# A fused attention and mixer kernel: the table of positions that sets its order, with other numbers

## The chip, the cores and the metric

The kernel runs on 1 core of one Trainium2 chip. The metric is the device time in microseconds (us) of one execution. The kernel before was timed three times: 1544.9, 1541.44 and 1538.11 us, a median of 1541.44 us. The profiled execution is a separate one, and its own time stands in the table below.

## The reference

What must be computed, for 8 batches of 448 positions, 12 heads of 64 and a model width of 768:

```python
scores = matmul(q, k.T) / sqrt(64) - log(448)
attn   = sigmoid(scores)
x      = concat_heads(matmul(attn, v))          # 448 x 768 per batch
h      = x.T @ U @ V                            # rank 32, mixes the positions
u      = x + h.T
out    = u + relu(u @ w_ch1) @ w_ch2            # 768 -> 3072 -> 768
```

There is no softmax, so scores, sigmoid and values of a pair of heads follow each other without a reduction over the row.

## The kernel before, in words

**Attention** of a batch is done in six pairs of heads (`pair`). Scores are matmuls at L578 and, for the last 64 rows of two pairs together, at L582. ScalarE (ACT) takes the sigmoid from PSUM at L706. The values are matmuls at L597 and L607, and VectorE (DVE) copies them out at L752. Batches 0 to 3 and 7 take the scores in float32, the others as pairs of float16 numbers; for those a scale is found by sending two columns to memory and back (`far`, `row`).

**Mixing** (`mix`, `mix_half`): the largest value of three columns of tiles is reduced on DVE (`mm_x`), spread over the partitions by a TensorE transposition (L451), made into a scale by short DVE instructions, and the columns are split into two float16 parts on ACT, GpSimd (POOL) and DVE (`xst`). One DMA transposes them (L893, `xst<-xst`), seven matmuls multiply by U (L901), ACT and DVE take the result (`xnt`), and three matmuls multiply by V (L911).

**The feed-forward part** of batches 0 and 1 (`ffn_in`, `ffn_out`) runs over six groups of hidden columns. A chain of 18 matmuls at L990 makes one tile of hidden values, ACT reads it twice (L997 and L998, relu), DVE takes the difference (L999), and chains of 12 matmuls at L1010 multiply by the second matrix. The weights come as 64-bit numbers. `decode` turns each of the 12 weight blocks into two float16 parts: four DMAs, several DVE and ACT instructions for each of four pieces (L432, L435, L484, L495), a largest value (`mm_w`, L919) that TensorE spreads (L451), and conversions by ACT or POOL (L959) and DVE (L435). The 12 `mm_w` transpositions on TensorE are called **marks** 1 to 12 below. Here mark 3 is the first with the name `mm_w__173`, and a later one has that name again, since three buffers are used in turn.

**Batches 2 to 7** are multiplied in pairs by a scheme of seven products instead of eight, all at L1198.

**The order** is made by a planner when the program is built. Every operation is put down with an engine, a cost, the operations that it needs, and a position `pos`. `Plan.order` then goes forward in planned time: at each step the engine that can begin first takes, of the operations that are ready, the one with the smallest position. Each engine executes its instructions in that order and waits in place where one isn't ready. Positions are sums of the constants at L66 to L74: where a batch's attention starts against the feed-forward groups (`BEFORE`, `AHEAD`, `LATER_AT`), how far values trail scores (`VALUES`, `SECOND`), where the mixing stands (`MIXED`, `MIX_2`), and how far decoding runs ahead (`DECODE`). Buffers are handed out in the planned order too. Two constants are not positions: `BOND` is an advantage in position for a TensorE operation that goes on in the array tiling in use (full, 64 rows, 64 columns, or 64 by 64), and `LATE` is added to the time at which the operations of attention and mixing count as ready on TensorE (for the feed-forward chains it is 0.3).

The line that makes an operation ready, `x[5]` being that slack:

```python
at = told + x[5] if x[0] != e or e == "SP" else end[i] + (0.0 if e == "PE" else 0.14)
```

Of the kernel before, what the change touches and what calls it, by code (L numbers as in the profile page):

```python
# [58 lines left out]
LATER = [2, 3, 4, 5, 6, 7]  # L59
FORMS = {1: (0, 1, 2)}  # L60
MM = 0.1893
SWITCH, BOND = 0.11, 41.647
T32_N = 3
PIPE, LANDS, LATE = 0.32e6, 3.237, -3.383

ROOM0, ROOM, AHEAD, BEFORE, PACE = 181.648, 286.578, -68.264, 91.805, 0.05  # L66
LATER_AT = 266.225
PREP, BOUNDS, VALUES, SECOND, MIXED = 137.851, 20.1, -1.552, 1.83, -5.728
MIXED1, MIX_1 = 4.915, 99.976
MIX_2, EV_IN, EV_OUT, A_OFF = 111.691, 64.755, 39.267, -86.102  # L70
START, DECODE = 280.941, 151.107
U_AT, U_STEP = 14.793, 3.625
LEAD, SUMS, STEP_K, STEP_I, FFN_LEAD = 17.258, 175.507, 40.462, 27.17, -42.823
W_AT, W_STEP, PAIR0, MIX0A, MIX0B, W2_LAG, G0_LEAD = -164.381, 28.657, 21.251, 146.75, -434.739, 1.269, 6.128  # L74
LOW_G = 1
FB = 8
SHIFT = dict()
# [165 lines left out]
def fused_kernel(ctx: ExitStack, tc: tile.TileContext, q, k, v, wu, wv, w1, w2, out):  # L243
# [1079 lines left out]
    def units(n):  # L1323

        b = min(n // NG, PLAIN - 1)
        step = (BEGIN[b + 1] - BEGIN[b]) / NG
        at = BEGIN[b] + (n - b * NG) * step
        nf = ne = 0
        for x in PATTERN:
            if x == "i":  # L1330
                if n < len(slots):
                    ffn_in(*slots[n], nf, at)
                nf += 1
                at += step * 18 / 144
            else:
                if n:
                    ffn_out(*slots[n - 1], ne, at)
                ne += 1
                at += step * 12 / 144

    def attention(b, start, d):
        new_u(b)
        for p in range(NP):
            pair(b, p, start + d * p, d)
            if b >= WHOLE and p in (3, 5):
                mix_half(b, p // 5, start + (MIXED - 5 + p) * d)
        if b < WHOLE:
            mix(b, 0.0, start + MIXED1 * d)

    for n, (b, g) in enumerate(slots):  # L1350
# [15 lines left out]
        if n == NG - 1:  # L1366
            d = PACE * (BEGIN[1] - BEGIN[0]) / 7.6
            attention(1, BEGIN[0] - BEFORE, d)
            d = (BEGIN[PLAIN] - AHEAD - BEGIN[0] - LATER_AT) / (NP * len(LATER) + 0.5)
            for j, x in enumerate(LATER):  # L1370
                attention(x, BEGIN[0] + LATER_AT + NP * d * j, d)
            attended = [len(plan.ops) - 1]
            FORMS_AT, FORMS_STEP = BEGIN[0] + LATER_AT + NP * d * U_AT, U_STEP
    units(len(slots))
# [88 lines left out]
```

## Time and profile before

| what | before |
|---|---|
| median of three runs | 1541.44 us |
| the profiled execution's own time | 1536.72 us |
| its span, first to last instruction | 1534.9 us |
| mean granted TensorE clock | 0.998 |
| DVE, ACT, POOL busy, share of the span | 67%, 43%, 19% |
| mean busy share of the DMA engines' time, queue 1 | 62.6% |

The profiled execution takes 1.8 us more than its span. Matmuls are pipelined, and their ends are modelled, so busy time of TensorE (PE) says when it has something in the array, not that it is at its peak. One matmul with 448 columns of float16 starts 189 ns after the one before it where nothing interferes; a float32 matmul stands as two records in the trace and as one row in the order. "Idle before" in a row is time in which the engine stood still just before it, with what ended that.

### The profile page before, as it was taken

The numbers are of one execution on the slowest core, as the hardware profiler recorded it, in microseconds if no ns is written. First come the engines' busy times: TensorE is split into PE (matmuls) and PEld (weight loads), VectorE is DVE, ScalarE is ACT, GpSimd is POOL, SyncE is SP. The second block draws the span as 40 slices with busy tenths as digits, with TensorE's granted clock in tenths as the row PEclk, the third lists the DMA queues.
The fourth block names the chain that finished last, engine by engine and source line by source line (L and its number), as shares of the span: only waits on it lengthen the run. The fifth ranks groups of instructions, "written<-read, shape, count | busy, mean of one in ns | idle before, by whom it ended". The sixth has DMA issues, their size and how long they took to land.

```text
span 1534.9 us, 22014 instructions
## 1 busy us (share of the span) xinstructions
PE 1512.8 (99%) x8194; PEld 731.6 (48%) x8194; DVE 1030.8 (67%) x1788; ACT 662.9 (43%) x1060; POOL 287.6 (19%) x352
## 2 busy tenths in 40 slices
PE   8999999999999999999999999999999999999999
PEld 3344544434444444445555555555555555555554
DVE  3789887755577756468776768665656757565656
ACT  5677787454465656434242352421223413121310
POOL 0100000444565220002546452000000400000000
PEclk9999999999999999999999999999999999999999
DMA  8788778985877997686766576533335373433331
GB/s 226 244 253 261 281 241 312 296 267 165 198 219 195 236 215 200 215 242 231 249 226 226 191 244 207 181 120 103 119 116 187 117 256 119 123 119 109 108 108 73
DMA packets 202188, 299.18 MB, mean 195 GB/s; under 512 B 52832, under 2 KB 158944, under 8 KB 199008
## 3 DMA queue, kind: packets, MB, share of 16 engines
q1 hardware_dynamic: 202080, 297.77, 62.6%
q8 instruction: 64, 1.05, 0.3%
q14 instruction: 44, 0.36, 0.1%
HBM read 226.20 MB, written 63.23 MB: 189 GB/s over the span
## 4 chain that ended last, share of the span: by engine, by line
PE 90%; DMA 5%; DVE 2%; ACT 2%; issue 1%; SPq 0%; ACTq 0%
PE banks L1198 56%; PE banks L1010 9%; PE banks L990 9%; PE banks L597 6%; PE banks L578 5%; PE banks L607 1%; PE banks L582 1%; DMA xst<-xst 1%; PE banks L901 1%; DMA far<-ss__203 1%; ACT a L706 1%; DMA row__110<-far 1%; DMA qk__99<-k_in 1%; DMA w<-w_in 1%; DMA forms<-xnt 1%
## 5 line engine op out<-in xcount | busy, mean ns | idle before, releaser
L1198 PEld LDWEIGHTS <-w__89 128*128 128x128 f16 x1197 | 117.1, 98 | 109.1
L1198 PEld LDWEIGHTS <-w__91 128*128 128x128 f16 x1134 | 111.0, 98 | 104.1 <-issue 0.8
L1198 PEld LDWEIGHTS <-w__90 128*128 128x128 f16 x1134 | 111.0, 98 | 103.5
L1198 PEld LDWEIGHTS <-w__92 128*128 128x128 f16 x1071 | 104.8, 98 | 97.8
L706 ACT ACTIVATE a<-banks,bias_s 128x896 f32<-128x896 f32 x105 | 99.1, 1007 | 58.9 <-PE banks L578 58.9
L1054 POOL TENSOR_TENSOR w<-w 128x384 f32<-128x384 f32 x96 | 102.0, 1063 | 5.2
L1010 PE MATMUL banks<-h__94,w__92 128*128 128x448 f16 x432 | 86.2, 353 | 0.0
L1010 PE MATMUL banks<-h__93,w__91 128*128 128x448 f16 x432 | 85.9, 353 | 0.0
L990 PE MATMUL banks<-us__87,w__90 128*128 128x448 f16 x432 | 85.0, 353 | 0.5 <-DVE ub__82 L435 0.5
L990 PE MATMUL banks<-us__87,w__89 128*128 128x448 f16 x432 | 84.9, 353 | 0.0
L1050 POOL TENSOR_TENSOR w<-w 128x384 f32<-128x384 f16 x48 | 45.2, 971 | 120.2 <-DVE xnt L1062 88.2
L1010 PEld LDWEIGHTS <-w__91 128*128 128x128 f16 x432 | 41.1, 98 | 45.2 <-issue 8.1
L1010 PEld LDWEIGHTS <-w__92 128*128 128x128 f16 x432 | 41.3, 98 | 44.0 <-issue 7.4
L990 PEld LDWEIGHTS <-w__90 128*128 128x128 f16 x432 | 41.6, 98 | 42.6 <-issue 5.7
L990 PEld LDWEIGHTS <-w__89 128*128 128x128 f16 x432 | 41.6, 98 | 40.7 <-issue 3.6
L1198 PE MATMUL banks<-a,w__89 128*128 128x448 f16 x267 | 60.2, 352 | 0.0
L1198 PE MATMUL banks<-a,w__91 128*128 128x448 f16 x255 | 56.7, 352 | 0.0
L1198 PE MATMUL banks<-a,w__90 128*128 128x448 f16 x249 | 56.2, 352 | 0.0
L1198 PE MATMUL banks<-a,w__92 128*128 128x448 f16 x237 | 53.5, 352 | 0.0
L1155 POOL TENSOR_TENSOR h__94<-w 128x448 f32<-128x448 f32 x2 | 2.3, 1138 | 256.6 <-ACT xst L1158 256.1
L435 DVE SCALAR_TENSOR_TENSOR stg<-w,stg 128x768 int32<-128x768 int32 x48 | 45.2, 955 | 7.5 <-ACT stg L484 7.2
L1050 POOL TENSOR_TENSOR w<-w__89 128x384 f32<-128x384 f16 x16 | 14.4, 925 | 183.6 <-DVE t L435 168.8
(1271 smaller groups left out, 3172.0 us busy)
## 6 DMA issues: line engine op xcount, KB each, us to landing
w<-w_in SPq DMA_DIRECT2D x48, 768.0 KB, 6.0
forms<-xnt SPq DMA_DIRECT2D x24, 768.0 KB, 4.8
w__89<-forms SPq DMA_DIRECT2D x19, 768.0 KB, 5.6
w__90<-forms SPq DMA_DIRECT2D x18, 768.0 KB, 4.9
w__91<-forms SPq DMA_DIRECT2D x18, 768.0 KB, 5.6
w__92<-forms SPq DMA_DIRECT2D x17, 768.0 KB, 5.5
w<-kept SPq DMA_DIRECT2D x12, 768.0 KB, 5.1
w__89<-kept SPq DMA_DIRECT2D x43, 192.0 KB, 3.0
```

The source lines that it names most:

```text
L435: nc.vector.scalar_tensor_tensor(out=out, in0=in0, scalar=s, in1=in1, op0=op0, op1=op1)
L578: nc.tensor.matmul(sc[j].x[:, h, :S], x[rows_of(h), j * P : j * P + P], y[rows_of(h)], start=i == 0, stop=i == n - 1)
L582: nc.tensor.matmul(sc[j].x[rows_of(m), h, :S], x[rows_of(h), 3 * P : S], y[rows_of(h)], start=i == 0, stop=i == n - 1)
L597: nc.tensor.matmul(av.x[rows_of(h), :S], x[:, j, rows_of(h)], y(tiles[j], h), start=j == 0 and i == 0, stop=not quad and j == 2 and i == n ...
L607: nc.tensor.matmul(avs[m].x[rows_of(h), :S], x[rows_of(m), rows_of(h)], y(tiles[3], h)[rows_of(m)], start=False, stop=i == n - 1, skip_gro ...
L706: act(cost, lambda: nc.scalar.activation(out_(), in_(), AF.Sigmoid, bias=bias_s, scale=c if ws else by.x), kin + ["bias"] + ([] if ws else ...
L901: nc.tensor.matmul(tp.x[:, :384], m.rearrange("p a b -> p (a b)"), x[:, j], start=j == 0, stop=j == 6)
L990: nc.tensor.matmul(ph.x[:, :S], w.x[:, f, c, x], us.x[:, c, y, :], start=c == 0 and i == 0, stop=c == NP - 1 and i == 2,)
L1010: nc.tensor.matmul(po.x[:, :S], w.x[:, f, e, x], h.x[:, f, y, :], start=f == 0 and i == 0, stop=f == FC - 1 and i == 2,)
L1050: pool(0.93, lambda j=j: nc.gpsimd.tensor_tensor(out=t.x[:, j], in0=quarter(j, 0), in1=quarter(j, 1), op=ALU.add), [w] if b is None else k ...
L1054: pool(1.0, lambda o_=o_, x=x, y=y, sub=sub: nc.gpsimd.tensor_tensor(out=t.x[:, o_], in0=t.x[:, x], in1=t.x[:, y], op=ALU.subtract if sub ...
L1198: nc.tensor.matmul(bank.x[:, :S], wt[1](k, n, x), both(f)[:, y], start=start and k == i == 0, stop=k == 2 and i == 2, skip_group_check=True)
```

## The change

Thirty-five of the constants get other numbers; nothing else differs. The program has the same operations with the same buffers, in another order on each engine.

```diff
-SWITCH, BOND = 0.11, 41.647
+SWITCH, BOND = 0.11, 41.69
 T32_N = 3
-PIPE, LANDS, LATE = 0.32e6, 3.237, -3.383
+PIPE, LANDS, LATE = 0.32e6, 3.237, -0.319
...
-ROOM0, ROOM, AHEAD, BEFORE, PACE = 181.648, 286.578, -68.264, 91.805, 0.05
+ROOM0, ROOM, AHEAD, BEFORE, PACE = 214.557, 284.256, -78.391, 110.251, 0.231
...
-START, DECODE = 280.941, 151.107
+START, DECODE = 330.869, 184.368
```

What this moves is seen in the order of TensorE. Rows of the order name the line, the operation and the tiles; "x6" is six in a row.

**First place: the beginning of the feed-forward part, mark 3.** Before, the values of the last pairs of batch 1 (L597 and L607 with `v__104`) and the first chain at L990 stand ahead of mark 3:

```order
L597 MATMUL banks<-a,v__104 64x448 x6
L607 MATMUL banks<-a,v__103 64x448 x2
L607 MATMUL banks<-a,v__104 64x448 x2
L990 LDWEIGHTS w__89
L990 MATMUL banks<-us__87,w__89 128x448
...
L451 MATMUL banks<-ident,mm_x__184 128x128
L451 MATMUL banks<-ident,mm_w__173 128x128
```

Now:

```order
L597 MATMUL banks<-a,v__103 64x448 x6
L451 MATMUL banks<-ident,mm_w__173 128x128
L990 LDWEIGHTS w__89
L990 MATMUL banks<-us__87,w__89 128x448
...
L597 MATMUL banks<-a,v__104 64x448 x6
L607 MATMUL banks<-a,v__103 64x448 x2
L607 MATMUL banks<-a,v__104 64x448 x2
```

One chain of 18, the values of one pair and the shared rows of two pairs, and the transposition of `mm_x__184` went behind the mark.

**Second place: the scale of batch 1's feed-forward part** (`mm_u__154`, which needs a PSUM bank that ACT has read at L998). Before, two operations of scores stand between the chain at L990 and it:

```order
L990 LDWEIGHTS w__89
L990 MATMUL banks<-us__87,w__89 128x448
L578 MATMUL banks<-qk__100 128x448 x2
L578 MATMUL banks<-qk__98 128x448 x4
L451 MATMUL banks<-ident,mm_u__154 128x128
L597 MATMUL banks<-a,v__101 64x448 x6
```

Now chains of the second matrix stand ahead of it, 24 matmuls of them with mark 10 in their middle:

```order
L1010 LDWEIGHTS w__92
L1010 MATMUL banks<-h__94,w__92 128x448
L1010 LDWEIGHTS w__92
L1010 MATMUL banks<-h__94,w__92 128x448
L451 MATMUL banks<-ident,mm_u__154 128x128
L597 MATMUL banks<-a,v__101 64x448 x6
```

The transposition moved behind those chains, and the scores of the next pair behind it.

**Third place: the second half of batch 3's mixing**, the matmuls at L901 that need the transposing DMA. Before, chains at L1010 with `w__92` stand right ahead of them:

```order
L1010 LDWEIGHTS w__92
L1010 MATMUL banks<-h__94,w__92 128x448
L901 LDWEIGHTS ua
L901 MATMUL banks<-xst,ua 128x384
...
L901 LDWEIGHTS vraw
L901 MATMUL banks<-xst,vraw 128x384
L578 LDWEIGHTS stg
```

Now:

```order
L1010 LDWEIGHTS w__92
L1010 MATMUL banks<-h__94,w__92 128x448
L990 LDWEIGHTS w__89
L990 MATMUL banks<-us__87,w__89 128x448
...
L990 LDWEIGHTS w__89
L990 MATMUL banks<-us__87,w__89 128x448
L901 LDWEIGHTS ua
L901 MATMUL banks<-xst,ua 128x384
```

A whole chain of 18 at L990 came between; from the transposition of `mm_x__185` down to there the two orders are otherwise alike.

More of the change, by code (lines that the diff above doesn't have):

```diff
@@ L61 @@
 MM = 0.1893
-SWITCH, BOND = 0.11, 41.647
+SWITCH, BOND = 0.11, 41.69
 T32_N = 3
-PIPE, LANDS, LATE = 0.32e6, 3.237, -3.383
-ROOM0, ROOM, AHEAD, BEFORE, PACE = 181.648, 286.578, -68.264, 91.805, 0.05
[L67 to L70, printed above, removed]
-START, DECODE = 280.941, 151.107
-U_AT, U_STEP = 14.793, 3.625
-LEAD, SUMS, STEP_K, STEP_I, FFN_LEAD = 17.258, 175.507, 40.462, 27.17, -42.823
-W_AT, W_STEP, PAIR0, MIX0A, MIX0B, W2_LAG, G0_LEAD = -164.381, 28.657, 21.251, 146.75, -434.739, 1.269, 6.128
+PIPE, LANDS, LATE = 0.32e6, 3.237, -0.319
+ROOM0, ROOM, AHEAD, BEFORE, PACE = 214.557, 284.256, -78.391, 110.251, 0.231
+LATER_AT = 299.257
+PREP, BOUNDS, VALUES, SECOND, MIXED = 95.44, 41.748, -2.303, 4.224, -3.369
+MIXED1, MIX_1 = 9.912, 128.223
+MIX_2, EV_IN, EV_OUT, A_OFF = 102.651, 51.643, 14.955, -54.012
+START, DECODE = 330.869, 184.368
+U_AT, U_STEP = 11.751, 9.413
+LEAD, SUMS, STEP_K, STEP_I, FFN_LEAD = 4.655, 183.86, 134.948, 92.753, -61.381
+W_AT, W_STEP, PAIR0, MIX0A, MIX0B, W2_LAG, G0_LEAD = -156.961, 34.804, 22.742, 243.826, -385.102, 1.228, -18.991
 LOW_G = 1
```

## The prediction

> **What bounds the kernel now.** First the page: its sums and the chain that ended last.
>
> ```profile
> span 1534.9 us, 22014 instructions
> PE 1512.8 (99%) x8194; PEld 731.6 (48%) x8194; DVE 1030.8 (67%) x1788; ACT 662.9 (43%) x1060; POOL 287.6 (19%) x352
> ...
> PE 90%; DMA 5%; DVE 2%; ACT 2%; issue 1%; SPq 0%; ACTq 0%
> ```
>
> The reader is to see that TensorE is the bound: 99% busy, and 90% of the chain. The matmuls are the same in both programs, so an order can only change three things: the 22 us in which TensorE stands still (1534.9 - 1512.8), the time that it runs at a lower clock, and the small price of going from one array tiling to another. Next, the busy time by stage, here two rows of it.
>
> ```profile
> core 0: us, PE busy (x) PEld busy (x) DVE busy (x) ACT busy (x) POOL busy (x), PEclk, DMA share, GB/s
> 95.00:171.00 76.00, 74.43 (x409) 39.15 (x406) 72.14 (x130) 53.46 (x93) 2.14 (x2) 1.00 0.81 274
> ...
> 670.00:1535.00 865.00, 860.76 (x4552) 445.18 (x4549) 569.04 (x925) 255.43 (x441) 136.90 (x133) 1.00 0.50 163
> ```
>
> From 670 us on TensorE loses 865.0 - 860.8 = 4.2 us in all, nearly all of it the end of the span. The matmuls of L1198 stand there in both programs, nearly in the same order apart from the buffers' numbers, so I expect nothing won or lost. Everything is decided in the first 670 us. In the first row DVE is busy for 72.1 of 76 us: while the weights are decoded, DVE is about as full as TensorE. Third, who TensorE waits for:
>
> ```profile
> PE banks L578 <- DMA qk__98<-q_in: 4.2, 1, 4.2
> PE banks L901 <- DMA xst<-xst: 3.1, 2, 2.8
> PE banks L816 <- ACT xnt L815: 2.0, 2, 1.4
> PE banks L451 <- ACT h__93 L998: 1.6, 1, 1.6
> PE banks L911 <- DVE xnt L435: 1.3, 1, 1.3
> PE banks L451 <- DVE mm_w__171 L919: 1.0, 1, 1.0
> PE banks L578 <- ACT a L706: 0.9, 2, 0.7
> PE banks L578 <- DMA qk__100<-q_in: 0.9, 1, 0.9
> PE banks L578 <- DVE ub__81 L752: 0.8, 1, 0.8
> PE banks L597 <- ACT h__93 L998: 0.5, 1, 0.5
> ...
> PE banks L597 <- DVE ub__81 L435: 0.4, 1, 0.4
> PE banks L451 <- ACT a L706: 0.2, 1, 0.2
> PE banks L578 <- DVE ub__85 L752: 0.2, 1, 0.2
> ```
>
> The columns are the total, how often, and the longest. The first 20 DMAs and the first matmuls stand in the same order in both programs, so 4.2 and 0.9 us at the start stay. The 2.0 us at L816 stay too: the copies by ACT there have as little TensorE work ahead of them as before.
>
> **What goes: the wait at the third place.** Rows of TensorE, then the DMA in the chain, then all twelve transposing DMAs from issue to landing:
>
> ```profile
> 386.68 0.27 PE L451 MATMUL banks<-ident,mm_x__185 128*128 128x128 f32 x1
> ...
> 397.25 2.43 PE L1010 MATMUL banks<-h__94,w__92 128*128 128x448 f16 x12
> 402.46 1.12 PE L901 MATMUL banks<-xst,ua 128*128 128x384 f16 x3 [2.77 <-DMA xst<-xst]
> ```
>
> ```profile
> 393.18 9.23 DMA xst<-xst
> ```
>
> ```profile
> DMA to landing us min/median/max: 5.0/5.3/9.2
> ```
>
> This DMA took 9.2 us where the median is 5.3, and TensorE, done at 399.7 us, waited 2.8 us. The new order puts a chain of 18 at L990 there: 18 x 0.189 = 3.4 us of work, more than the wait. Over all twelve such places the TensorE work between the transposition of `mm_x` and L901, added up from the order with start distances like that 0.189 us, goes from 10.4 to 16 us (one of 26) to 12 to 20 us (one of 24): so -2.8 us here, and -0.3 us at the other place that waited. The chain that moved up isn't needed to cover L901 to L911 later: 3.4 us of work lie between them here now, as at the place that waited 1.3 us for `xnt`, while places with 2.7 us did not wait. I take that wait as 0 (it stays or moves; -1.3 to +1.3).
>
> **What goes: the half speed behind two waits.** The same view in short stretches:
>
> ```profile
> 220.00:225.00 5.00, 3.49 (x11) 1.26 (x13) 4.97 (x10) 5.00 (x9) 0.00 (x0) 0.66 0.98 339
> 400.00:405.00 5.00, 2.54 (x9) 0.97 (x10) 1.91 (x2) 0.00 (x0) 3.50 (x4) 0.75 0.99 222
> 405.00:410.00 5.00, 5.00 (x30) 2.19 (x26) 2.56 (x4) 2.09 (x2) 3.82 (x8) 0.91 0.96 321
> ```
>
> The granted clock (the number ahead of the last two) falls behind both longer waits: 5 x 0.34 = 1.7 us of work are lost at 220 us, and 5 x 0.25 + 5 x 0.09 = 1.7 us at 402 us. With the wait of 2.8 us its 1.7 us should go: **-4.8 us** for the third place and its like.
>
> Here a page speaks against this. The Trainium skill, in "TensorE: Matmul & The Clock Gate", section on HAM oscillation, gives the rule as no idle gaps over about 3.4 us. This trace does not agree: waits of 2.8 and 1.6 us had a stretch at half speed behind them. By the page neither wait would be its cause, and 3.4 us less would be saved; that is the second rival below.
>
> **What goes: the wait at the second place.** TensorE, then ACT:
>
> ```profile
> 217.75 1.67 PE L578 MATMUL banks<-qk__98 64*128 64x448 f32 x8
> 220.98 0.32 PE L451 MATMUL banks<-ident,mm_u__154 128*128 128x128 f32 x1 [1.56 <-ACT h__93 L998]
> 221.84 4.01 PE L597 MATMUL banks<-a,v__101 128*64 128x448 f32 x12 [0.53 <-ACT h__93 L998]
> ```
>
> ```profile
> 215.34 2.57 ACT L959 ACTIVATE w__92<-t,s_w__182 128x768 f16<-128x768 f32 x3
> ...
> 220.41 0.52 ACT L998 ACTIVATE h__93<-banks 128x448 f16<-128x448 f32 x1
> ```
>
> ACT was busy converting `w__92`, so the relu that frees the bank came late. The order of ACT is nearly the same there now, but between mark 9 and `mm_u__154` TensorE has some 25 us of work where it had 6. So 1.6 + 0.5 us of waiting and 1.7 us of half speed go: **-3.8 us**, or nothing if another bank is late.
>
> **What goes: short waits.** With a larger `LATE`, operations stand further behind what they need. Counted over both orders, with TensorE work added up as above: 39 score operations and 21 value operations had under 2 us of TensorE work behind the matmul on which, over one instruction of ACT or DVE, they depend; now 24 and 7, so 31 in place of 60. The rows of this kind (0.9, 0.8, 0.4, 0.2, 0.2) sum to 2.5 us; half of it goes, **-1.2 us** (between -2.5 and +2.5: fewer such pairs can still wait longer).
>
> **What comes: more changes of tiling.** The order has 219 changes from one array tiling to another before, 233 now. Two chains of 18, from the chain that ended last, one behind values (L607), one behind a chain of the same tiling:
>
> ```profile
> 338.90 3.51 PE banks L990 x18
> ```
>
> ```profile
> 166.02 3.40 PE banks L990 x18
> ```
>
> That is 0.11 us each, and 14 x 0.11 = **+1.5 us**.
>
> **What comes: mark 3 too early.** TensorE, then DVE:
>
> ```profile
> 93.02 2.42 PE L597 MATMUL banks<-a,v__104 128*64 128x448 f32 x12
> ...
> 96.29 3.58 PE L990 MATMUL banks<-us__87,w__89 128*128 128x448 f16 x18
> ...
> 99.82 0.27 PE L451 MATMUL banks<-ident,mm_w__173 128*128 128x128 f32 x1
> ```
>
> ```profile
> 95.51 0.15 DVE L919 TENSOR_REDUCE mm_w__173<-ssw__170 128x1 f32<-128x4 f32 x1
> ```
>
> DVE had the value at 95.7 us, TensorE asked for it at 99.8. The work from 93.0 to 99.8 us, without 0.1 for `mm_x`, goes behind the mark, so TensorE comes to it at 93.1. The DVE instructions ahead of the value add up to the same in both orders within 1 us (each by the mean of its kind), so it comes at about 95.5 again. TensorE waits 95.5 - 93.1 = **+2.4 us** (0 if DVE, with fewer waits of its own, is 2.4 us sooner). Behind the mark nothing is behind it in the queue that could go first: L990 and the values stand still with it. Whether that is won back depends on DVE, since the stretch that follows is the one with 72.1 of 76 us: between marks 3 and 9 both orders have 109 to 110 us of TensorE work and the same DVE work within 1 us, so I let it take the same time. At mark 9 DVE had its value at 210.2 us, and TensorE asked for it at 213.3:
>
> ```profile
> 210.00 0.16 DVE L919 TENSOR_REDUCE mm_w__173<-ssw__170 128x1 f32<-128x4 f32 x1 [0.47 <-ACT w L495]
> ```
>
> ```profile
> 213.29 0.27 PE L451 MATMUL banks<-ident,mm_w__173 128*128 128x128 f32 x1
> ```
>
> At marks 7 to 9 DVE's work is 5, 2 and 0 us less than before where TensorE's is 9, 6 and 8 us less; this bounds the term at 8 us less the 3.1 us by which DVE was ahead at mark 9, so 0 to +4.9.
>
> **Sum.** -4.8 - 3.8 - 1.2 + 1.5 + 2.4 = -5.9 us against the profiled execution's 1536.72, which gives 1530.8. The runs' median of 1541.44 lies 4.7 us above that execution, so the same difference gives **1535.5 us**. In DMAs and other engines nothing is hidden that wasn't: the queue of SP issues the same transfers, and those ahead of the first 90 rows only trade places.
>
> **The rivals.** *All the margin is real and DVE keeps up:* no wait at mark 3, all short waits gone, `xnt` too: -4.8 - 3.8 - 2.5 - 1.3 + 1.5 = -10.9, 1530.5 us. For it: ten of the twelve distances to L901 grow, all of the short ones, and scores stand further behind. Against: full DVE at 95 to 171 us. *The half speed isn't due to the waits* (by the page's rule): -5.9 + 3.4, 1538.9 us. For it: two cases only; against: both directly behind a wait. *The waits only move:* nothing but the changes of tiling, +1.5, 1543 us. An order that fits one execution's transfers can miss another's; the runs differ by 7 us among themselves. *Slower, by DVE at marks 7 to 9:* TensorE comes 4.9 us too early, in three waits of over 1.5 us, each with 1.7 us of half speed behind it: 4.9 + 5.1 + 1.5, and the relu behind ACT's conversions is late as before (no -3.8); -4.8 and -1.2 still come: +5.5, 1546.9 us. It decides from waits of 1.6 us on, the shortest with half speed behind it. Against it: the 42 us between marks 7 and 9 had DVE idle for 8.
>
> **The numbers.** Forecast 0.37, all margin real 0.29, half speed not due to waits 0.08, waits only move 0.14, DVE slower 0.12. The range takes 1530.5 less 3 us, since a median of three moved by 3 us either way, and 1546.9: 1527 to 1547. A measurement of this kernel tells about 0.5%, 7.7 us: faster means under 1533.7, slower over 1549.1. Faster: the second case and a quarter of the first, 0.38. Slower: most of the last, 0.09. Same: 0.53.
>
> **What would show it.** In the new profile: no wait of L901 on `xst` over 1 us; granted clock 1.00 from 20 to 1500 us; `mm_u__154` without idle time; mark 3 with a wait of about 2.4 us on `mm_w__173`; idle TensorE of some 16 us in place of 22. It is wrong if new waits of over 1.5 us stand between 300 and 670 us, or if the clock falls at marks.

## The result and the profile after

| | before | changed |
|---|---|---|
| median of 20 runs | 1543.92 us | 1533.82 us |
| lowest to highest | 1537.85 to 1550.65 us | 1531.12 to 1542.57 us |
| ratio | | 0.9938 (95% interval 0.9923 to 0.9952) |
| ratio, in a second measurement (e2 below) | | 0.996 (0.9939 to 0.9982) |

The forecast of 1535.5 us against 1541.44 us is a ratio of 0.9961. The gain is real and, in the first measurement, larger than forecast: some 9.6 us in place of 5.9. The second measurement holds the forecast within its interval.

Two things must be known before the profiles are compared. The profiled execution of the changed kernel took 1542.57 us, the slowest of its 20 runs; the profiled execution of before took 1536.72 us, faster than every one of its 20 runs. So the two profiles, laid side by side, say the opposite of the runs. Both kernels were therefore profiled again (e1 and e2). First the page of the changed kernel, first profile, then the waits of TensorE in the second profile of each kernel: total, how often, longest.

```profile
span 1540.8 us, 22051 instructions
PE 1521.5 (99%) x8194; PEld 731.5 (47%) x8194; DVE 1036.3 (67%) x1788; ACT 664.2 (43%) x1060; POOL 291.0 (19%) x352
```

Second profile of before:

```profile
PE banks L901 <- DMA xst<-xst: 7.8, 4, 3.4
PE banks L578 <- DMA qk__98<-q_in: 4.3, 1, 4.3
PE banks L816 <- ACT xnt L815: 2.0, 2, 1.4
PE banks L911 <- DVE xnt L435: 1.9, 1, 1.9
PE banks L451 <- ACT h__93 L998: 1.5, 1, 1.5
PE banks L451 <- DVE mm_w__171 L919: 1.0, 1, 1.0
```

Second profile of the changed kernel:

```profile
PE banks L578 <- DMA qk__98<-q_in: 4.3, 1, 4.3
PE banks L578 <- DVE ub__81 L752: 1.9, 2, 1.3
PE banks L804 <- ACT a L706: 1.9, 1, 1.9
PE banks L582 <- ACT a L706: 1.5, 2, 1.2
PE banks L578 <- DMA qk__100<-q_in: 1.3, 1, 1.3
PE banks L901 <- DMA xst<-xst: 1.0, 2, 0.6
...
PE banks L597 <- ACT a L706: 0.8, 2, 0.4
```

The reader is to see that the wait for the transposing DMA, 3.1 us in the first profile of before, is 7.8 us in the second, and 1.0 us in the changed kernel (0.8 in its first profile). The wait of L451 on `h__93`, the second place, is there again in before and gone in the changed kernel. But the changed kernel has new waits on ACT's sigmoids (`a`) and on DVE's copies (`ub`). What each stage gains and loses is seen in the busy time: before (second profile), then the changed kernel (second profile).

```profile
0.00:97.00 97.00, 89.81 (x444) 33.62 (x445) 61.15 (x115) 64.41 (x90) 7.14 (x17) 1.00 0.82 237
97.00:278.00 181.00, 177.29 (x941) 87.77 (x939) 155.02 (x279) 131.71 (x214) 7.07 (x8) 0.99 0.80 272
278.00:670.00 392.00, 380.06 (x2212) 161.62 (x2211) 240.23 (x463) 210.48 (x315) 137.45 (x195) 0.99 0.79 213
```

```profile
0.00:97.00 97.00, 87.17 (x411) 32.82 (x413) 62.53 (x112) 62.56 (x89) 7.80 (x17) 0.96 0.82 235
97.00:278.00 181.00, 181.00 (x974) 89.14 (x971) 161.24 (x287) 136.36 (x217) 10.05 (x10) 1.00 0.81 275
278.00:670.00 392.00, 385.30 (x2260) 163.19 (x2258) 241.77 (x465) 208.74 (x315) 138.92 (x192) 1.00 0.80 219
```

TensorE's busy time (first number behind the length) and the granted clock (third from the right) tell it: the changed kernel is worse in the first 97 us, without a gap in the next 181 us, and better behind 278 us.

Busy time leaves out the price of changes of tiling and what half clock costs. So the loss of a stretch was also worked out from the trace: the time from its first matmul to its end, less the sum of the nominal start distances of its matmuls (0.189 us for 448 columns of float16, and for the other kinds what stands between two of them in the trace where nothing interferes). The stretches end at the first chain of L990 and at the first `mm_x__185`; both orders have done nearly the same work there. "Half" is how long the clock stood at one half in the first two stretches and behind them, without the last few us of the span.

```
us lost                       to 1st L990   to 1st mm_x__185   behind it   half, first two | behind
before, first profile             19.8             9.4            33.8            3.4 | 3.4
before, second (e1)               20.1            10.0            42.1            3.4 | 10.2
changed, first profile            32.4             4.2            32.2           20.5 | 0
changed, second (e2)              25.8             4.2            33.7            6.8 | 0
```

The clock is given for every run too, so the mean span can be split into what half clock cost (span times 1 less the clock) and the rest:

```
                         runs   mean span   lost to half clock   rest
before, beside e1 to e4   28     1544.0           7.3           1536.7
changed (e2)              11     1536.7           4.2           1532.5
```

Of the 7.3 us between the two means, 3.1 are half clock, and 4.2 are the rest, waits and changes of tiling among it. The first 20 runs of the changed kernel have a mean span of 1532.6 us, 3.6 of it lost to half clock and 1529.0 the rest.

### The profile page after: what moved, and what is told of

It is laid out like the page before. It is cut to its first block, busy times and chain, and to the rows that moved or that the text cites. A ratio compares the mean times of both kernels' runs of the same rounds, so it can differ in the third digit from the quotient of the medians.

```text
span 1540.8 us, 22051 instructions
## 1 busy us (share of the span) xinstructions
PE 1521.5 (99%) x8194; PEld 731.5 (47%) x8194; DVE 1036.3 (67%) x1788; ACT 664.2 (43%) x1060; POOL 291.0 (19%) x352
## 4 chain that ended last, share of the span: by engine, by line
PE 87%; DMA 7%; ACT 2%; DVE 2%; issue 1%; SPq 1%; POOL 0%; ACTq 0%; POOLq 0%; DVEq 0%
PE banks L1198 56%; PE banks L990 8%; PE banks L1010 8%; PE banks L597 5%; PE banks L578 5%; DMA w<-parked 1%; DMA row__110<-far 1%; PE banks L582 1%; PE banks L607 1%; DMA w<-w_in 1%; DMA qk__98<-q_in 1%; SPq L408 1%; DMA qk__100<-q_in 1%; ACT a L706 1%; PE banks L901 1%
## 5 line engine op out<-in xcount | busy, mean ns | idle before, releaser
L1198 PEld LDWEIGHTS <-w__89 128*128 128x128 f16 x1197 | 117.1, 98 | 109.2
L1198 PEld LDWEIGHTS <-w__91 128*128 128x128 f16 x1134 | 110.9, 98 | 104.2 <-issue 0.8
L1198 PEld LDWEIGHTS <-w__90 128*128 128x128 f16 x1134 | 111.0, 98 | 103.5
L1198 PEld LDWEIGHTS <-w__92 128*128 128x128 f16 x1071 | 104.8, 98 | 97.8
L1010 PE MATMUL banks<-h__93,w__91 128*128 128x448 f16 x432 | 86.4, 353 | 0.3 <-DVE ub__82 L435 0.3
L1010 PE MATMUL banks<-h__94,w__92 128*128 128x448 f16 x432 | 86.5, 353 | 0.0
L990 PE MATMUL banks<-us__87,w__90 128*128 128x448 f16 x432 | 85.4, 353 | 0.0
L990 PE MATMUL banks<-us__87,w__89 128*128 128x448 f16 x432 | 84.7, 353 | 0.0
L1010 PEld LDWEIGHTS <-w__92 128*128 128x128 f16 x432 | 41.0, 98 | 45.0 <-issue 8.7
L1010 PEld LDWEIGHTS <-w__91 128*128 128x128 f16 x432 | 41.1, 98 | 43.8 <-issue 7.9
L990 PEld LDWEIGHTS <-w__90 128*128 128x128 f16 x432 | 41.5, 98 | 41.9 <-issue 4.9
L990 PEld LDWEIGHTS <-w__89 128*128 128x128 f16 x432 | 41.8, 98 | 40.6 <-issue 2.8
L1198 PE MATMUL banks<-a,w__91 128*128 128x448 f16 x273 | 59.0, 352 | 0.0
L1198 PE MATMUL banks<-a,w__89 128*128 128x448 f16 x255 | 56.9, 352 | 0.0
L1198 PE MATMUL banks<-a,w__90 128*128 128x448 f16 x234 | 51.8, 352 | 0.0
L1198 PE MATMUL banks<-a,w__92 128*128 128x448 f16 x228 | 50.6, 352 | 0.0
L435 DVE SCALAR_TENSOR_TENSOR t<-w,t 128x768 int32<-128x768 int32 (+1 forms) x49 | 45.2, 942 | 1.7 <-ACT t L484 0.9
```

The source lines that it names most:

```text
L435: nc.vector.scalar_tensor_tensor(out=out, in0=in0, scalar=s, in1=in1, op0=op0, op1=op1)
L990: nc.tensor.matmul(ph.x[:, :S], w.x[:, f, c, x], us.x[:, c, y, :], start=c == 0 and i == 0, stop=c == NP - 1 and i == 2,)
L1010: nc.tensor.matmul(po.x[:, :S], w.x[:, f, e, x], h.x[:, f, y, :], start=f == 0 and i == 0, stop=f == FC - 1 and i == 2,)
L1198: nc.tensor.matmul(bank.x[:, :S], wt[1](k, n, x), both(f)[:, y], start=start and k == i == 0, stop=k == 2 and i == 2, skip_group_check=True)
```

## The experiments

All have the operations and buffers of before. Ratios are to the kernel before on the same chip; e1 to e4, e5 to e8 and e9 to e12 ran on three different chips.

**e1 and e2: both kernels again.** No edit.

> The kernel before, unchanged, for a second profile and for the granted clock of several executions. Theory 1 (the same few waits cost time in every execution): the wait of L901 on the transposing DMA and that of mm_u__154 stand in this profile too, at about 2.8 and 1.6 us, each with a stretch at half clock. Theory 2 (the first profile was one draw, and transfers fall unevenly): waits of this size stand at other places, and the clock of the executions spreads from 0.993 to 1.0. Ratio to the kernel before 1.000.

> The changed kernel, unchanged, for a second profile: the first one, at 1542.57 us, is 8.75 us over the median of its 20 runs, with 20.5 us at half clock in its first 90 us. Expected a span near 1532 us, ratio 0.992 to 0.996, less half clock in the first 95 us. At mark 3, theory A (the forecast's step): a wait of about 2.4 us on mm_w__173, which the slow beginning hid in the first profile. Theory B: DVE, with fewer waits of its own, has the value in time, no wait over 0.5 us.

Measured: e1 1545.4 us, ratio 1.0 (0.998 to 1.0019); e2 1538.86 us, ratio 0.996 (0.9939 to 0.9982). Both theories of e1 are right in part: both waits of the forecast came again at the same places (3.4 us for L901 at 405 us, 1.5 us for `mm_u__154`), and others came beside them (2.4 and 1.8 us for L901 at 473 and 555 us). At mark 3 there is no wait in e2, as theory B said, but for another reason: DVE's value came at 98.2 us, later than in e1 (95.8), and TensorE, after a longer beginning, only at 99.2 us.

**e3: the two waits alone.** Six moves in the order of before; rows of this kernel carry line numbers 5 higher from L236 on.

```diff
+MOVES = [(2291, 1219), (675, 544), (680, 691), (681, 691), (954, 691), (963, 691)]
...
-        for i in self.order():
+        done = self.order()
+        for i, j in MOVES:
+            done.remove(i)
+            done.insert(done.index(j), i)
+        for i in done:
```

> The kernel before with its two largest waits covered by six moves in its order and nothing else: one chain of L990 goes ahead of the matmuls of L901 at the third place, and on ACT the relu L998 that frees the bank of mm_u__154, the next relu pair and two sigmoids go ahead of weight conversions at the second place. Theory 1 (these waits and the half clock behind them are the gain): 8.6 us less, ratio 0.9944. Theory 2 (other waits of other executions count as much, and only distance everywhere helps): 0 to 4 us less, ratio 0.9975 to 1.000.

Measured: 1544.41 us, ratio 1.0001 (0.9978 to 1.0024). Theory 1 falls. Both waits are gone, and both came back one step later. At the second place, TensorE and then DVE:

```profile
219.74 0.32 PE L456 MATMUL banks<-ident,mm_u__154 128*128 128x128 f32 x1
...
227.66 4.83 PE L1015 MATMUL banks<-h__94,w__92 128*128 128x448 f16 x24 [3.33 <-DVE e_u__157 L459]
```

```profile
222.70 0.96 DVE L440 SCALAR_TENSOR_TENSOR stg<-w,stg 128x768 int32<-128x768 int32 x1 [2.16 <-ACT stg L489]
...
223.64 2.69 DVE L440 SCALAR_TENSOR_TENSOR stg<-w,stg 128x768 int32<-128x768 int32 x3
226.25 0.62 DVE L1004 TENSOR_TENSOR h__93<-r__95,h__93 128x448 f16<-128x448 f32 x1
226.78 0.62 DVE L1004 TENSOR_TENSOR h__93<-r__96,h__93 128x448 f16<-128x448 f32 x1
227.32 0.28 DVE L459 TENSOR_REDUCE e_u__157<-banks 128x1 f32<-128x128 f32 x1
```

`mm_u__154` no longer waits. But the bank that it fills is read by `e_u__157`, which stands on DVE behind four instructions of decoding and two differences of hidden values (7.6 us after the transposition), and the next chain of L1010 (L1015 here) needs that bank. DVE stood still for 2.2 of the 7.6 us, behind ACT, which by the moves has the sigmoids to do first. So 2.1 us of waiting became 3.3. At the third place the chain that now covers L901 no longer stands behind it, and waits on sigmoids (0.7 and 0.3 us) and one of 1.9 us on `xnt`, at 418 us, took the place of the 2.8.

**e4: `LATE` alone.** The number that makes TensorE's operations stand further behind what they need, with the positions of before.

```diff
-PIPE, LANDS, LATE = 0.32e6, 3.237, -3.383
+PIPE, LANDS, LATE = 0.32e6, 3.237, -0.319
```

> The kernel before with LATE = -0.319 alone, all positions left as they were. Score and value operations with under 2 us of TensorE work behind their producer go from 60 to 36, the distances to L901 from 10.3 to 26 us to 13.1 to 26 us, the changes of tiling up by 21. Theory 2 (distance everywhere is the gain): 6 to 10 us less, ratio 0.9935 to 0.996. Theory 3 (the gain comes from where the feed-forward part and decoding start, START, DECODE and BEFORE): 0 to 2 us more by the 21 changes of tiling at 0.11 us, ratio 1.000 to 1.0015.

Measured: 1572.21 us, ratio 1.0191 (1.0161 to 1.022), 17.8 us of it lost to half clock. Neither theory had this. The largest wait, TensorE and then DVE:

```profile
536.54 1.31 PE L578 MATMUL banks<-stg 64*128 64x448 f16 x6 [5.38 <-DVE ub__83 L752]
```

```profile
533.72 0.42 DVE L468 TENSOR_REDUCE e_qkv__205<-row__110 128x2 f32<-128x256 f32 x1 [3.77 <-DMA row__110<-far]
...
535.88 0.62 DVE L752 COPY ub__83<-banks 128x448 f32<-128x448 f32 x1
```

DVE stood still for 3.8 us for the two columns that come back from memory, and the copy that TensorE needs was queued behind it and behind another instruction that waited 1.1 us for ACT. Distance counted in TensorE work says nothing of what is ahead in the other engine's queue.

**e5 to e8 and e12: stretches exchanged.** The order is given as a list, made of the two kernels' own orders: all operations up to the cut from one, what is left from the other. Buffers are handed out along it. Where the two orders meet is called the seam below.

```diff
-        t = Tile(name, buffers, in_turn)
+        t = Tile(name, buffers, False)
...
+            i = next((i for i in GIVEN if not left[i] and room(i) is not None), None)
+            GIVEN.remove(i)
+            o, r = self.ops[i], room(i)
+            e = o[0]
+            t = max(free[e], ready[i], r[0] + o[5] if r[1] else 0.0, port if o[8] else 0.0, landed[-8] if e == "SP" else 0.0)
```

> Order of the kernel before up to the first chain of L990 (the first 96 us), from there the order of the changed kernel. Both orders have done nearly the same work at that point. TensorE's loss over its nominal start distances was 20 us in that stretch before and 26 to 32 us after, 10 and 4 us from there to the first mm_x__185, and 34 to 42 and 32 to 34 us behind it. Theory S (the stretches add up; the change loses 6 us or more in the beginning and wins behind it): ratio to the kernel before 0.990 to 0.993, 6 us or more below the changed kernel. Theory L (what the beginning loses is needed, since it lets DVE run ahead for the marks behind it): a wait of about 2 us and more at mark 3 or behind it, and no gain over the changed kernel, ratio 0.995 to 0.997.

> The reverse: order of the changed kernel up to the first chain of L990, from there the order of the kernel before. Theory S: 6 us or more above the kernel before, ratio 1.004 to 1.007. Theory L: 0 to 2 us above it or below it, ratio 0.999 to 1.001, with less waiting at marks 4 to 9.

> Order of the changed kernel only from the first chain of L990 to the first mm_x__185 (about 96 to 278 us), that of the kernel before on both sides. Theory S: the loss of this stretch goes from 10 to 4 us, ratio 0.996; mm_u__154 waits no more. If the second place's gain moves elsewhere: ratio 0.999 to 1.001.

> Order of the kernel before up to the first mm_x__185 (about 278 us), that of the changed kernel behind it. This stretch holds all twelve waits of L901 on its DMA, which took 2.8 us in the first profile of before and 7.8 us in the second. Theory S: 2 to 8 us below the kernel before, ratio 0.995 to 0.999. If the waits there only move: ratio 1.000.

Measured: e5 1541.73 us, 0.9988 (0.997 to 1.0005); e6 1546.62 us, 1.0004 (0.9991 to 1.0018); e7 1553.07 us, 1.005 (1.0031 to 1.0068); e8 1544.75 us, 0.9993 (0.9977 to 1.001). Theory S, that stretches add up, falls in e5, e6 and e7; theory L is right in kind, though e5 came out slower than it said. e5, the beginning of before with the marks of the changed kernel: TensorE, then what DVE made for mark 4 (mark 3, at 96.61 us, did not wait, since the values with `v__104` stand ahead of it here).

```profile
96.77 13.78 PE L990 MATMUL banks<-us__87,w__89 128*128 128x448 f16 x72
117.09 0.48 PE L451 MATMUL banks<-ident,mm_w__171 128*128 128x128 f32 x1 [6.54 <-DVE mm_w__171 L919]
```

```profile
L919 DVE TENSOR_REDUCE mm_w__171<-ssw__168 x1: 157/157/157, 120.2 to 120.2; 128x1 f32<-128x4 f32 x1
```

The second fence is mark 4 in the second profile of before: DVE starts its value at 120.2 us there. In e5 TensorE is at the mark at 110.6 us and DVE's value comes at 117.0: 6.5 us of waiting, and 10.2 us of half clock from the same place on. But DVE was not full ahead of it. ACT, then DVE in e5:

```profile
100.98 0.99 ACT L484 ACTIVATE stg<-w,minus 128x768 f32<-128x768 uint16 x1 [3.46 <-DMA w<-w_in]
```

```profile
102.00 0.96 DVE L435 SCALAR_TENSOR_TENSOR stg<-w,stg 128x768 int32<-128x768 int32 x1 [5.45 <-ACT stg L484]
```

Between the marks DVE stood still for 5.5 us behind an ACT instruction that itself waited 3.5 us for a transfer of weights; why the transfer came late is open. In e2 this instruction does not wait, DVE's value is there at 114.8 us, and TensorE, after its longer beginning, comes to mark 4 at 116.4. So part of what the changed kernel loses in the first 97 us is time in which decoding, transfers and ACT included, catches up; without it as much is lost at the mark. e7 has the same wait (6.0 us, with DVE idle for 4.9 us in the same way) and 17.1 us of half clock ahead of it; e8 has 5.9 us of new losses at its seam, from 281 to 306 us (1.2, 0.4, 3.2 and 1.1).

> Order of the changed kernel up to the first mm_x__185 (about 280 us), that of the kernel before behind it: what the first 280 us give by themselves. TensorE lost 29 to 30 us there in both kernels of the undisturbed profiles, so if the whole gain lies behind it the ratio is 0.999 to 1.001; if the first 280 us hold half of it, 0.9965 to 0.998. The waits of L901 on its DMA should be back at about 7 us.

Measured: 1545.1 us, 0.9996 (0.9974 to 1.0018). The first 280 us of the changed kernel, followed by the order of before, give nothing, and the waits of L901 are back at 9.2 us. But this kernel too has 4.1 us of new losses at its seam (2.8 and 1.3 us at 278 and 284 us), and e8, which has only the other part of the change, gives nothing either. So the times of these runs alone don't say which part holds the gain. The traces do: worked out as in the table above, the stretch behind the first `mm_x__185` loses 33.9 us in e5, which has the changed order there, and 40.3 us in e6 and in e7, which have that of before. No run puts one kernel's whole order through this list, but the first 96 us, with the order of before, lose 20.2 us in e5 and 19.9 in e8, as they do in before (19.8 and 20.1).

**e9 to e11: the distance to the transposing DMA by itself.** Only the matmuls of L901 get another slack: -0.319 (e9) and 1.5 (e10) in the kernel before, -3.383 in the changed kernel (e11).

```diff
-        pe(1.2, mixed, [xt, "ux"] + KUA, [tp], pos + 2.0)
+        pe(1.2, mixed, [xt, "ux"] + KUA, [tp], pos + 2.0, 1.5)
```

> The kernel before with one number more: the matmuls of L901 alone get a slack of -0.319 in place of -3.383. The order of the first 278 us stays as it was; behind it the twelve distances to L901 go from 10.3 to 26 us to 11.0 to 19 us. Theory D (the gain of the stretch behind 278 us is the distance to the transposing DMA): waits of L901 on it from about 7 us in all to 2 to 4, ratio to the kernel before 0.996 to 0.9985. Theory M (the waits only move, to xnt and the sigmoids): ratio 0.9995 to 1.002.

> The same with a slack of 1.5: all twelve distances are 14.4 to 21 us. Theory D: waits of L901 on its DMA under 1.5 us in all, ratio 0.995 to 0.9975, below the run with -0.319. Theory M: 0.9995 to 1.002 in both.

> The changed kernel with the slack of L901 alone put back to -3.383; its distances go from 12 to 25 us to 8.3 to 21 us. Theory D: waits of L901 on its DMA of 3 us or more, 3 to 6 us above the changed kernel, ratio to the kernel before 0.998 to 1.000. Theory M: as the changed kernel, 0.994 to 0.997.

Measured: e9 1552.83 us, 1.0055 (1.003 to 1.0079); e10 1547.4 us, 1.0017 (0.9995 to 1.0039); e11 1553.87 us, 1.0051 (1.0029 to 1.0073). First e11: the waits and the largest one.

```profile
PE banks L901 <- DMA xst<-xst: 15.3, 5, 6.1
```

```profile
499.82 1.12 PE L901 MATMUL banks<-xst,ua 128*128 128x384 f16 x3 [6.13 <-DMA xst<-xst]
```

Taking the distance away from the changed kernel costs 0.0091 of the time against e2 (each by its ratio to before), some 14 us, with 15.3 us of waiting on that DMA: more than theory D expected. Here the distance is needed. In e9 and e10 no wait of L901 on its DMA is left, as theory D said, and no time is won, as theory M said; e9 is even slower than theory M's range, and why stays open. e10's waits of over 2 us, the DMA at the start left out:

```profile
PE banks L1198 <- DMA w__89<-forms: 4.6, 1, 4.6
...
PE banks L451 <- ACT a L706: 2.8, 1, 2.8
PE banks L582 <- ACT a L706: 2.5, 2, 1.6
```

Waits on sigmoids took the place of those on `xst`. The 4.6 us on a transfer of L1198's weights, at 934 us, are new too; no run tells whether the moved matmuls cause them.

## Why the prediction was right, and where its steps were not

**The third place: right, and sized too small.** The changed kernel has 0.8 and 1.0 us of waits of L901 on its DMA where before has 3.1 and 7.8, and no half clock behind 278 us where before has 3.4 and 10.2 us of it. The mean of the two profiles gives 4.6 us of waits and, at half of 6.8 us, 3.4 us of half clock: 8 us in place of the 4.8 of the sum. The term was mis-sized because it took one profiled execution as typical, one that was faster than any of 20 runs. e11 shows that the distance is needed; e9 and e10 that it isn't enough. What is needed beside it wasn't separated: in the changed kernel the sigmoids, the scales and the second half of the mixing are placed anew as well.

**The second place: right in the whole order.** `mm_u__154` has no idle time ahead of it in both profiles of the changed kernel, and the stretch from the first L990 to the first `mm_x__185` loses 4.2 us where it lost 9.4 and 10.0. By itself no run shows it to be worth anything: moved alone, the wait comes back as 3.3 us in the queues of DVE and ACT (e3), and without the longer beginning the stretch waits 6.0 us at mark 4 (e7).

**Mark 3: the wrong place and engine.** The forecast let the first 97 us stand but for 2.4 us at mark 3 ("The first 20 DMAs and the first matmuls stand in the same order in both programs", "the 2.0 us at L816 stay too"). This holds to about 23 us. From there on the order differs, and the changed kernel loses 25.8 us where before loses 19.8 and 20.1 (e6, e11 and e12, with the same beginning, 26.8, 22.4 and 23.1). The largest new piece in the second profile:

```profile
51.94 0.33 PE L804 MATMUL banks<-ident,ua__78 128*128 128x128 f32 x1 [1.93 <-ACT a L706]
```

ACT's rows say why: an instruction of decoding stands still 5.17 us for its weights, and the two sigmoids that free the bank are queued behind it.

```profile
50.01 0.98 ACT L484 ACTIVATE t<-w,minus 128x768 f32<-128x768 uint16 x1 [5.17 <-DMA w<-w_in]
50.90 1.89 ACT L706 ACTIVATE a<-banks,bias_s 128x896 f32<-128x896 f32 x2
```

In the second profile of before the same kind of instruction stands behind the sigmoid (47.57 us), begins at 49.95 us and stood still 0.62 us. The forecast compared what stands ahead of L816 in TensorE's work and not what stands ahead of the sigmoids in ACT's queue. The four beginnings have a mean of 24.5 us, 4.4 us over the 20.1 of e1 (the first profile's 32.4, with 20.5 us of half clock, is left out): in place of +2.4 at the mark, +4.4 ahead of it. Of this, 2.1 us are half clock: the four have 6.8, 6.8, 0 and 3.4 us of it there, and e1 none. A spell that begins at 82 to 91 us stands in four of the five profiles with this beginning, 1.6 to 3.2 us behind a wait of 0.8 or 0.9 us at L842, and in none of the other nine, which don't have that wait. What is left, +2.3, is near the 2.4 forecast for another place and engine, which is luck. That decoding sets when the marks can go is borne out by e5: 6.5 us at mark 4, over the bound of 4.9. That a full DVE does it is not: DVE stood still for 5.5 us ahead of that mark, behind ACT and a transfer. The forecast's 93.1 us for mark 3 is 0.1 us too late, since `mm_x` went behind the mark too; nothing hangs on it.

**Short waits: the wrong sign. Tilings: not separated.** Waits of score and value matmuls and of L451 on a sigmoid or on `ub` add up to 2.5 and 2.1 us in the two profiles of before, and to 3.7 and 5.4 us in the two of the changed kernel: +2.3 on the mean in place of -1.2, near the upper bound of +2.5 that the forecast gave. e4 had nearly the count of close pairs of the changed kernel (36; 31 there) and was 27 us slower. That count was no measure of waiting.

**The sum.** Beginning +4.4, to the first `mm_x__185` -5.5 (4.2 less the mean 9.7 there), behind it -5.0 (mean 33.0 less mean 38.0): -6.1 us. Behind it 8 us of waits and half clock went and the stretch won 5.0, so some 3 us of other losses came; the short waits and the changes of tiling are among them, and they were not split further. The forecast said -5.9, with smaller terms on both sides; the runs of e2 gave 7.3 in the mean span, the first 20 runs 9.6 by their ratio (the mean span of the two profiles of before is 4.5 us under that of its 28 runs, so their losses are on the low side). The errors, a DMA wait sized too small and a beginning and short waits costed too low, cancelled. That the waits of the second and third place would go was foreseen; that the sum came so close was luck. What stays open is why the first measurement won some 3 us more than the second; in the changed kernel it is little of it half clock (3.6 us of the mean span in the first, 4.2 in the second), and the intervals overlap.

**The signs.** As forecast, the changed kernel has no wait of L901 on `xst` over 1 us and no idle time at `mm_u__154`. The wait at mark 3 and a clock of 1.00 from 20 us on did not come, and TensorE was idle for 19.3 and 20.7 us in the two profiles, not 16. The first has a wait of 1.52 us on a sigmoid at 524 us, just over the 1.5 us at which the forecast called itself wrong.

**The rivals.** "The waits only move" is what each part does alone (e3, e9, e10), and not what the whole does. "Slower, by DVE" has its wait at mark 4, once the beginning is undone (e5), though ACT and a transfer hold DVE up there. "The half speed isn't due to the waits" is taken up below.

## What to carry to other kernels

An order is one piece: in three of three tries (e3, e9, e10), covering a wait of some us at one place won no time. In e3 it came back one step later, since the engine that is late there has other work queued ahead; in e9 and e10 others came. Look for what stands ahead in the queue of the engine that is waited for, and for what that engine waits for in turn, not only at the distance in TensorE work. And take more than one profile before pricing a wait of some us: here the first profile of before was faster than all its 20 runs, and that of the changed kernel the slowest of its own.

## What the runs showed of the hardware

**Half clock begins on a grid.** In 14 profiles the clock's record has 55 spells at half speed; every one begins a whole multiple of 3.413 us after the record's first entry, and all but those cut off by the end last 1, 2, 3, 4 or 5 such steps. The grid lies elsewhere against the program in each execution. So a wait doesn't fix what follows: the same wait of 1.56 us at `mm_u__154` has a stretch at half speed behind it in the first profile of before, and none in e10, and the 3.33 us of e3 have none either.

```profile
223.89 0.32 PE L451 MATMUL banks<-ident,mm_u__154 128*128 128x128 f32 x1 [1.56 <-ACT h__93 L998]
```

```profile
220.00:225.00 5.00, 2.90 (x15) 1.21 (x15) 5.00 (x9) 5.00 (x9) 0.00 (x0) 1.00 0.36 104
225.00:230.00 5.00, 5.00 (x30) 1.61 (x27) 4.29 (x9) 5.00 (x9) 0.00 (x0) 1.00 0.92 365
```

These are e10: clock 1.00 on both sides. The Trainium skill, in "TensorE: Matmul & The Clock Gate", section "What's actually happening", says that the window of 3413 ns is free-running and doesn't start with the kernel; the traces agree. The Trainium skill's section on HAM oscillation, on the same page, gives the limit as gaps of over about 3.4 us; the 1.56 us of before with half speed behind them don't agree. Whether half speed follows a wait changes from one execution to the next, so the 1.7 us that the forecast took for each was no sure price.

**The same transposing DMAs took 5.0 to 13.0 us from issue to landing** over the 14 profiles (medians 5.1 to 6.1), the longest in e8:

```profile
DMA to landing us min/median/max: 5.0/5.4/13.0
```

**Long half clock in the beginning belongs to neither order.** Stretches of 13.7 and 17.1 us at half speed, beginning 51 to 55 us after the record's first entry, stand in the first profile of the changed kernel, in e7 and in e9; the latter two have the beginning of before.
